# A branch hint for ScalarE at the jump past the general path

## The chip, the cores and the metric

The kernel runs on one core of a Trainium2 chip. The metric is the device time of one execution in microseconds, the median over runs. Before the change it was 179.29 us over 3 runs (179.23 to 179.44). The engines are named as the profile names them: PE is TensorE's matrix multiply and PEld its weight load, DVE is VectorE, ACT is ScalarE, POOL is GpSimd, SP is SyncE. A "q" behind a name (ACTq, SPq) is the engine's sequencer, which issues DMAs, reads registers, waits on semaphores and branches.

## The reference

Attention over 4 batches, 8 heads, 768 positions and a head size of 64. A flag for each head says whether it sees all earlier positions or only the first `n_sink` and the last `window`. The result goes through a feed-forward block that takes the larger of two products.

```python
mask = np.where(retr[0, :, 0, 0, None, None], full_mask, stream_mask)
scores = np.where(mask[None, :, :, :], scores, -1000000000.0)
scores = scores - np.max(scores, axis=-1, keepdims=True)
a = np.exp(scores)
a = a / (np.sum(a, axis=-1, keepdims=True) + 1e-09)
attn = np.matmul(a, v)
...
h1 = x @ w1
h2 = x @ w2
g = np.maximum(h1, h2)
return (g @ w_out).astype(np.float32)
```

Here three of the eight flags are set, `n_sink` is 4 and `window` is 64.

## The kernel before, in words

The program holds two versions of the computation. The special one, `tile_three_full_heads`, is right when exactly three heads see all positions and the row sums of the softmax stay in a sane range. The general one, `tile_any_heads`, is right for any flags. The special path always runs. At its end it writes a verdict of 0 or 1, and the general path runs only if the verdict is 0. With the inputs here the verdict is 1, so the general path's code is in the program and is jumped over.

The head of the program (L1657 to L1680) makes mask tables on POOL. ACT starts the DMA of the eight flags into `raw` (L1578, 64 bytes), and `head_order` sorts them on DVE into `found_i` (L1603), the heads in the order in which the special path takes them. The line L1677 reads those eight numbers into registers of POOL, DVE and ACT, since these three cast `q`, `k` and `v` from a head's place that a register names. The loads of `q`, `k` and `v` themselves bring all heads, are issued by SP and need no register.

The special path then runs through the four batches in halves of 384 positions: casts, transposes, scores (L953), exponentials (L972, ACT), masks (L991, DVE), weighted sums (L1016), normalising (L1043), then the feed-forward block (L1245 and L1302 on PE, L1270 on ACT and L1272 on DVE). The order on each engine is a plan written out by hand, so nothing in it moves when an instruction is put in elsewhere.

At the end the last output rows leave in two parts: 384 columns by a DMA of SP and 128 columns by a DMA of ACT (both L1327). PE adds up a test of the row sums (L1388), and DVE turns it into `verdict` in three small instructions (L1392, L1395, L1399). All five sequencers read `verdict` into a register (L1687) and branch on it (L1690). Behind the branch each engine waits for its own last work and gives a sign. SP walks through a list of semaphore waits, one after another, for all queues and engines. A barrier of the five engines then ends the program (these waits and the barrier carry L1727 in the profile, the line that closes the program).

The length of what is jumped over differs by engine. In the program's order PE has 3,566 instructions up to its branch and 13,744 in all; DVE 433 of 3,381; POOL 134 of 276; ACT 344 of 410; SP 114 of 116. On ACT the general path is 64 exponentials of L1518, besides the semaphore waits that they need.

A branch hint is an instruction of its own (BRANCH_PREFETCH_HINT), which names a branch that comes later and says that it will be taken. In the source `mark_branch_hint_location` names it by the label of the `If`. It stands near the end of the source, but the instruction is issued at the head of the engine's program, ahead of everything else.

Of the kernel before, what the change touches and what calls it, by code (L numbers as in the profile page):

```python
# [1574 lines left out]
def head_order(nc, small, is_retrieval, H):  # L1575

    raw = small.tile([1, 2 * H], I32, name="raw")
    nc.scalar.dma_start(  # L1578
        out=raw, in_=bass.AP(tensor=_as_int32(is_retrieval, 2 * H), offset=0, ap=[[0, 1], [1, 2 * H]])
    )  # L1580
    number = small.tile([1, H], F32, name="number")
    for h in range(H):
        nc.vector.memset(number[:, h:h + 1], float(H - h))
    flag = small.tile([1, 2 * H], F32, name="flag")
    r = small.tile([1, H], F32, name="r1")
    key = small.tile([1, H], F32, name="key")
    top = small.tile([1, H], F32, name="top")
    found = small.tile([1, H], F32, name="found")
    found_i = small.tile([1, H], I32, name="found_i")
    count = small.tile([1, 1], F32, name="count")  # L1590
    vec = nc.vector
    vec.tensor_single_scalar(out=flag, in_=raw, scalar=0.0, op=ALU.not_equal)
    two = flag.rearrange("p (h two) -> p h two", two=2)
    vec.tensor_tensor(out=r, in0=two[:, :, 0], in1=two[:, :, 1], op=ALU.max)
    vec.scalar_tensor_tensor(
        out=key, in0=r, scalar=2.0 * H, in1=number, op0=ALU.mult, op1=ALU.add
    )
    vec.max(out=top, in_=key)
    vec.tensor_scalar(
        out=key, in0=top, scalar1=2.0 * H, scalar2=-2.0 * H, op0=ALU.is_gt, op1=ALU.mult  # L1600
    )
    vec.tensor_tensor(out=key, in0=key, in1=top, op=ALU.add)
    vec.tensor_scalar(  # L1603
        out=found_i, in0=key, scalar1=-1.0, scalar2=float(H), op0=ALU.mult, op1=ALU.add
    )
    vec.tensor_reduce(out=count, in_=r, op=ALU.add, axis=AX.X)
    return found_i, count


def mask_table(nc, bias, n_sink, window):  # L1610

    at = lambda i, n=1: bias[:, 128 * i:128 * (i + n)]

    def put(i, n, base, by_key, by_query, fill=-1e30):
        nc.gpsimd.affine_select(
            out=at(i, n).rearrange("p (n c) -> p n c", c=128), in_=at(i, n).rearrange("p (n c) -> p n c", c=128),
            pattern=[[0, n], [by_query, 128]], compare_op=ALU.is_ge, fill=fill, base=base,
            channel_multiplier=by_key,
        )
    put(7, 1, 0, -1, 1)  # L1620
    put(0, 1, n_sink - 1, -1, 0)
    put(1, 2, window - 129, 1, -1)
    put(2, 1, -n_sink, 1, 0, 0.0)
    put(3, 3, window - 1, 1, -1)
    put(3, 1, -n_sink, 1, 0, 0.0)
    put(3, 3, 0, -1, 1)
    nc.gpsimd.tensor_copy(out=at(6)[0:64], in_=at(0)[0:64])
    nc.gpsimd.tensor_copy(out=at(6)[64:128], in_=at(1)[64:128])


@with_exitstack
def kernel(
    ctx: ExitStack,
    tc: tile.TileContext,
    q: bass.AP,
    k: bass.AP,
    v: bass.AP,
    is_retrieval: bass.AP,
    n_sink: int,
    window: int,  # L1640
    moe_w1: bass.AP,
    moe_w2: bass.AP,
    moe_w_out: bass.AP,
    out: bass.AP,
):
    nc = tc.nc
    B, H, S, D = q.shape
    n_sink, window = int(n_sink), int(window)
    assert D == 64 and S == 768 and H == 8
    ctx.enter_context(tc.manual_schedule())  # L1650
    anyhow = (q, k, v, is_retrieval, moe_w1, moe_w2, moe_w_out, out, n_sink, window)
    if not (1 <= window <= 64 and 0 <= n_sink <= 64):
        tile_any_heads(tc, *anyhow)
        return

    with tc.tile_pool(name="consts", bufs=1) as consts:
        tab = consts.tile([128, 16 * 128], BF16, name="tab")  # L1657
        lds = consts.tile([128, NLD, 3, H, S // 2 * D // 128], F32, name="ld")
        warm = consts.tile([128, 1], F32, name="warm")
        rez = consts.tile([128, B * H * S // 128], F32, name="rez")  # L1660
        verdict = consts.tile([1, 1], I32, name="verdict")
        warmer = consts.tile([128, 128], BF16, name="warmer")
        nc.gpsimd.memset(warmer, 0.0)
        nc.vector.memset(tab[:, 0:1152], 0.0)
        nc.gpsimd.affine_select(
            out=tab[:, 0:128], in_=tab[:, 0:128], pattern=[[1, 128]], compare_op=ALU.not_equal, fill=1.0,
            base=0, channel_multiplier=-1,
        )
        mask_table(nc, tab[:, 128:1152], n_sink, window)
        if K_BY_ACT:  # L1670
            nc.scalar.dma_start(
                out=lds[:, 0, 1], in_=k[0, :, 0:S // 2, :].rearrange("h (p n) d -> p h (n d)", p=128)
            )
        found, count = head_order(nc, consts, is_retrieval, H)
        nc.vector.memset(warm, 0.0)
        nc.scalar.activation(out=warm, in_=warm, func=ACT.Exp)
        _, heads = nc.values_load_multi_w_load_instructions(  # L1677
            found, engines=[nc.gpsimd.engine, nc.vector.engine, nc.scalar.engine], min_val=0, max_val=H - 1,
            skip_runtime_bounds_check_because="a permutation of the heads",
        )  # L1680
        tile_three_full_heads(
            tc, q, k, v, moe_w1, moe_w2, moe_w_out, out, tab, heads, rez, count,
            verdict, warmer, K_BY_ACT, lds,
        )
        tc.mark_branch_hint_location("other", hint="LikelyTaken",
            engines=[nc.tensor.engine, nc.vector.engine, nc.gpsimd.engine])
        right = nc.values_load(  # L1687
            verdict, min_val=0, max_val=1, skip_runtime_bounds_check_because="a product of two flags"
        )
    with tc.If(right < 1, label="other"):  # L1690
        tile_any_heads(tc, *anyhow)
# [40 lines left out]
```

## Time and profile before

| what | value |
|---|---|
| median of 3 runs | 179.29 us (179.23 to 179.44) |
| the profiled execution's own time | 179.4 us |
| its span, first to last instruction | 177.7 us |
| mean granted TensorE clock | 0.995 |
| DVE busy | 117.0 us (66%), 326 instructions |
| ACT busy | 124.5 us (70%), 279 instructions |
| POOL busy | 32.5 us (18%), 80 instructions |

The profiled execution took 1.7 us more than its span, and it lies 0.1 us above the median of the runs. Busy time counts only work in the engines themselves; a sequencer's waits, register reads and branches are not in it, but the views that list one source line show them with their durations and start times. Such a row reads: line, engine, operation, count, then shortest, median and longest duration in ns, then the start of the first and of the last in us.

### The profile page before, as it was taken

The numbers are of one execution on the slowest core, as the hardware profiler recorded it, in microseconds if no ns is written. First come the engines' busy times: TensorE is split into PE (matmuls) and PEld (weight loads), VectorE is DVE, ScalarE is ACT, GpSimd is POOL, SyncE is SP. The second block draws the span as 40 slices with busy tenths as digits, with TensorE's granted clock in tenths as the row PEclk, the third lists the DMA queues.
The fourth block names the chain that finished last, engine by engine and source line by source line (L and its number), as shares of the span: only waits on it lengthen the run. The fifth ranks groups of instructions, "written<-read, shape, count | busy, mean of one in ns | idle before, by whom it ended". The sixth has DMA issues, their size and how long they took to land.

```text
span 177.7 us, 4887 instructions
## 1 busy us (share of the span) xinstructions
PE 169.6 (95%) x1781; PEld 102.6 (58%) x1781; DVE 117.0 (66%) x326; ACT 124.5 (70%) x279; POOL 32.5 (18%) x80
## 2 busy tenths in 40 slices
PE   7999999999999999999999999999999999999970
PEld 7855655655756656666566447555554566545440
DVE  5448799878898787776777175786855578503130
ACT  3598716999698999999996879948475877132210
POOL 6860200320427310071001122000030000000000
PEclk9999999999999999999999999999999999999998
DMA  5999999999899998995959997549993261333040
GB/s 133 334 373 386 392 375 325 221 309 281 217 251 246 267 310 214 243 247 74 154 117 250 209 186 196 71 115 223 226 252 71 66 220 66 76 131 118 4 160 28
DMA packets 76654, 36.14 MB, mean 203 GB/s; under 512 B 59090, under 2 KB 70610, under 8 KB 76626
## 3 DMA queue, kind: packets, MB, share of 16 engines
q1 hardware_dynamic: 76480, 35.73, 78.5%
q8 instruction: 15, 0.25, 0.6%
q14 instruction: 13, 0.11, 0.2%
q10 hardware_dynamic: 146, 0.07, 0.1%
HBM read 25.17 MB, written 6.29 MB: 177 GB/s over the span
## 4 chain that ended last, share of the span: by engine, by line
PE 78%; DMA 7%; DVE 5%; ACT 2%; POOL 2%; issue 2%; DVEq 0%; SPq 0%; POOLq 0%; ACTq 0%
PE ps L1302 34%; PE ps L1245 21%; PE ps L953 9%; PE ps L1016 7%; DMA ld<-in_moe_w_out_dram 6%; PE ps L1222 3%; PE ps L674 3%; DVE at L991 1%; ACT at L972 1%; PE ps L1142 1%; POOL qb L378 1%; DMA raw<-in_is_retrieval_dram 1%; ACT wob L376 1%; POOL tab L606 1%; DVE vx L378 1%
## 5 line engine op out<-in xcount | busy, mean ns | idle before, releaser
L972 ACT ACTIVATE at<-ps 128x512 bf16<-128x512 f32 (+2 forms) x134 | 64.0, 576 | 6.7 <-PE ps L953 6.4
L1302 PE MATMUL ps<-wob,g 128*128 128x512 bf16 (+2 forms) x200 | 45.7, 371 | 0.0
L1245 PE MATMUL ps<-xt,w 128*128 128x384 bf16 x256 | 45.2, 326 | 0.0
L1245 PEld LDWEIGHTS <-w 128*128 128x128 bf16 x256 | 24.1, 98 | 16.5 <-issue 0.6
L991 DVE TENSOR_TENSOR at<-at,tab 128x1024 bf16<-128x1024 bf16 (+5 forms) x49 | 24.7, 519 | 12.4 <-ACT at L972 11.8
L1302 PEld LDWEIGHTS <-g 128*128 128x128 bf16 x200 | 18.2, 98 | 19.4 <-issue 0.2
L1272 DVE TENSOR_SCALAR g<-ps 128x384 bf16<-128x384 f32 x31 | 16.9, 552 | 14.7 <-PE ps L1245 14.3
L1302 PE MATMUL ps<-w2o,xt 128*128 128x512 bf16 (+2 forms) x100 | 24.7, 371 | 0.0
L1270 ACT ACTIVATE g<-ps 128x384 bf16<-128x384 f32 x33 | 15.9, 509 | 12.0 <-PE ps L1245 11.9
L1043 DVE TENSOR_TENSOR x<-ps,rez 128x192 f32 x64 | 22.6, 354 | 1.6
L378 POOL CAST qb<-ld 128x384 bf16 (+1 forms) x28 | 12.4, 476 | 57.3 <-DVE x L1043 19.8
L1016 PEld LDWEIGHTS <-at 128*128 128x128 bf16 x477 | 18.0, 97 | 6.1 <-DVE at L991 1.0
L376 ACT COPY ot<-ps 128x512 f32<-128x512 f32 (+1 forms) x16 | 9.1, 576 | 16.4 <-PE ps L1302 15.4
L1016 PE MATMUL ps<-vb,at 128*128 128x65 bf16 x387 | 19.3, 193 | 0.3 <-DVE at L991 0.2
L953 PE MATMUL ps<-qk 64*128 64x128 bf16 (+1 forms) x330 | 19.1, 228 | 0.0
L953 PEld LDWEIGHTS <-qk 64*128 64x128 bf16 x330 | 12.1, 94 | 9.3 <-issue 7.0
L376 ACT CAST qb<-ld 128x384 bf16 (+1 forms) x35 | 13.7, 451 | 4.5 <-DMA ld<-in_q_dram 3.3
L1302 PEld LDWEIGHTS <-xt 128*128 128x128 bf16 x100 | 8.9, 98 | 8.1
L378 DVE COPY qk<-ps 128x384 bf16<-128x384 bf16 (+1 forms) x14 | 9.6, 696 | 4.0 <-PE ps L674 3.6
L378 POOL CAST vb<-ld 128x192 bf16 x18 | 6.3, 385 | 28.7 <-DMA ld<-in_v_dram 26.6
L378 DVE COPY ot<-ps 128x512 f32<-128x512 f32 (+1 forms) x9 | 6.1, 673 | 8.0 <-PE ps L1302 8.0
L674 PE MATMUL ps<-tab,qb 128*128 128x128 bf16 x120 | 9.6, 219 | 0.5 <-POOL qb L378 0.3
(76 smaller groups left out, 162.9 us busy)
## 6 DMA issues: line engine op xcount, KB each, us to landing
out_dram<-ot SPq DMA_DIRECT2D x23, 256.0 KB, 2.6
ld<-in_v_dram SPq DMA_DIRECT2D x21, 256.0 KB, 5.2
ld<-in_moe_w_dram SPq DMA_DIRECT2D x4, 1024.0 KB, 12.1
ld<-in_q_dram SPq DMA_DIRECT2D x5, 768.0 KB, 8.2
ld<-in_k_dram SPq DMA_DIRECT2D x5, 768.0 KB, 7.8
ld<-in_q_dram SPq DMA_DIRECT2D x9, 256.0 KB, 5.1
ld<-in_k_dram SPq DMA_DIRECT2D x9, 256.0 KB, 4.6
ld<-in_moe_w_out_dram SPq DMA_DIRECT2D x4, 512.0 KB, 11.0
```

The costliest lines, as they stand in the source:

```text
L376: nc.scalar.copy(out=out, in_=in_)
L378: eng[e].tensor_copy(out=out, in_=in_)
L674: nc.tensor.transpose(to[:, i], qbs[:, T["qb", n, hf] % NQB, t, i].rearrange("p h d -> p (h d)"), ident)
L953: nc.tensor.matmul(to.rearrange("p (i c) -> p i c", c=128), lhsT=lhsT, rhs=q_of(n, i, m)[rows], start=bk not in under, stop=True, skip_gro ...
L972: nc.scalar.activation(out=at[:, bk, 0:w], in_=bank(("ps", b, hf, t), part=bk)[:, 0:w], func=ACT.Exp, scale=scale,)
L991: eng[e].tensor_tensor(out=at, in0=at, in1=tbl, op=ALU.mult)
L1016: nc.tensor.matmul(po[:, hh, i - NT * hf, :], lhsT=ats[:, T["at", b, hf, t] % NAT, bk, e * 128:(e + 1) * 128], rhs=rhs, start=first, stop= ...
L1043: nc.vector.tensor_tensor(out=xs[:, HALVES.index((b, hf)) % NX, :, bass.ds(heads[2 * p + hh], 1), :], in0=po[:, hh, :, 0:D].unsqueeze(2), ...
L1245: nc.tensor.matmul(bank(key)[:, 0:HALF], lhsT=w[:, kc, fc * 128:(fc + 1) * 128], rhs=xts[:, HALVES.index((b, hf)) % NXT, :, kc, :], start= ...
L1270: nc.scalar.activation(out=g, in_=ph, func=ACT.Relu)
L1272: nc.vector.tensor_scalar_max(out=g, in0=ph, scalar1=0.0)
L1302: nc.tensor.matmul(bank(key)[:, cols], lhsT=lhsT, rhs=(w2o if kind == "x" else wob)[:, c, cols], start=(e == 0), stop=(e == len(steps) - 1),)
```

## The change

One engine is added to the list of those that get the hint.

```diff
         tc.mark_branch_hint_location("other", hint="LikelyTaken",
-            engines=[nc.tensor.engine, nc.vector.engine, nc.gpsimd.engine])
+            engines=[nc.tensor.engine, nc.vector.engine, nc.gpsimd.engine, nc.scalar.engine])
         right = nc.values_load(
```

On ACT, at the head of the program, the order was this (the first branch enters the program; `raw` holds the flags, `warm` is a one-column tile that has the table of the exponential loaded early, `found_i` the sorted heads):

```order
L1727 UNCONDITIONAL_BRANCH
L1578 DMA raw<-in_is_retrieval_dram 1x16
L1676 ACT_TABLE_LOAD
L1676 ACTIVATE warm<-warm 128x1
L1677 TENSOR_LOAD found_i
```

And now, at the same place of ACT's program:

```order
L1727 UNCONDITIONAL_BRANCH
L1727 BRANCH_PREFETCH_HINT
L1578 DMA raw<-in_is_retrieval_dram 1x16
L1676 ACT_TABLE_LOAD
L1676 ACTIVATE warm<-warm 128x1
L1677 TENSOR_LOAD found_i
```

One instruction is new, ahead of the DMA of the flags, and everything behind it on ACT is one place later in the program. At the other end of ACT's program, where the branch itself stands, the rows are the same as before (`ot` is the last output tile):

```order
L376 COPY ot<-ps 128x128
L1327 DMA out_dram<-ot 128x128
L1687 TENSOR_LOAD verdict
L1690 COMPARE_AND_BRANCH
L1518 ACTIVATE any_a<-any_s 128x2304 x64
L1690 UNCONDITIONAL_BRANCH x2
```

Nothing moved there: ACT still jumps from the compare over the 64 exponentials. PE, DVE, POOL and SP run the same instructions in the same order as before.

## The prediction

> **What bounds the kernel now.** I looked first at where the busy time stops, then at what the sequencers do behind it. The page gives the span; the windows cut its end into pieces (each row: length, busy time and instructions of each engine, granted clock, DMA share, GB/s); the chain of waits gives the last piece of work.
>
> ```profile
> span 177.7 us, 4887 instructions
> ...
> 0.00:172.00 172.00, 169.58 (x1781) 102.59 (x1781) 116.60 (x323) 124.26 (x279) 32.50 (x80) 1.00 0.81 208
> 172.00:174.20 2.20, 0.00 (x0) 0.00 (x0) 0.43 (x3) 0.25 (x1) 0.00 (x0) 1.00 0.39 138
> 174.20:175.20 1.00, 0.00 (x0) 0.00 (x0) 0.00 (x0) 0.00 (x0) 0.00 (x0) 1.00 0.14 41
> 175.20:177.70 2.50, 0.00 (x0) 0.00 (x0) 0.00 (x0) 0.00 (x0) 0.00 (x0) 0.65 0.01 3
> ...
> 172.40 0.14 DVE verdict L1399
> ```
>
> Up to 172 us PE is busy 169.6 of 172.0, and the change touches none of that. The last work is DVE's verdict, over at 172.5. No engine computes in the 5.2 us that follow, and in the last 2.5 of them the DMAs are all but still too. So the question is what the sequencers do there. The views of the lines L1687 (register read) and L1690 (branch, and each engine's own wait behind it) show it.
>
> ```profile
> L1687 SPq TENSOR_LOAD <-verdict x1: 718/718/718, 172.6 to 172.6; - x1
> L1687 ACTq TENSOR_LOAD <-verdict x1: 555/555/555, 172.7 to 172.7; - x1
> ...
> L1690 POOLq EVENT_SEMAPHORE  x4: 17/43/43, 173.7 to 174.0; - x4
> L1690 POOLq COMPARE_BRANCH  x1: 65/65/65, 173.2 to 173.2; - x1
> L1690 DVEq COMPARE_BRANCH  x1: 84/84/84, 173.2 to 173.2; - x1
> L1690 ACTq COMPARE_BRANCH  x1: 54/54/54, 173.3 to 173.3; - x1
> L1690 SPq COMPARE_BRANCH  x1: 53/53/53, 173.4 to 173.4; - x1
> L1690 PEldq COMPARE_BRANCH  x1: 393/393/393, 173.4 to 173.4; - x1
> L1690 DVEq EVENT_SEMAPHORE  x1: 21/21/21, 173.9 to 173.9; - x1
> L1690 PEldq EVENT_SEMAPHORE  x1: 51/51/51, 173.9 to 173.9; - x1
> ...
> L1690 ACTq EVENT_SEMAPHORE  x1: 17/17/17, 176.7 to 176.7; - x1
> ```
>
> All five branch between 173.2 and 173.4. The three with a hint issue their next instruction 0.5 (POOL: 173.2 to 173.7), 0.7 (DVE) and 0.5 us (PE) later. ACT, without one, does so at 176.7, 3.4 us after its branch. It isn't held by the semaphore of that instruction: a wait shows up on ACT as a long record, as the next row says (1,913 ns for the longest), and this one is 17 ns long. ACT wasn't there yet.
>
> ```profile
> L376 ACTq EVENT_SEMAPHORE  x41: 17/17/1913, 17.8 to 170.0; - x41
> ```
>
> Who waits for ACT, the view of L1727 shows, asked for SP's walk in stretches and for the two engines that follow.
>
> ```profile
> L1727 SPq EVENT_SEMAPHORE  x12: 28/28/1912, 174.2 to 174.9; - x12
> ...
> L1727 SPq EVENT_SEMAPHORE  x1: 1912/1912/1912, 174.9 to 174.9; - x1
> ...
> L1727 SPq DRAIN  x2: 7/10/13, 176.8 to 176.9; - x2
> ...
> L1727 ACTq DRAIN  x2: 8/8/8, 176.8 to 177.1; - x2
> ...
> L1727 POOLq EVENT_SEMAPHORE  x4: 17/17/17, 176.9 to 177.6; - x4
> ```
>
> SP goes through 12 waits from 174.2 to 174.9 without a stop, 28 ns each, and stands at the twelfth for 1,912 ns, until ACT's sign at 176.7. Then come the barrier and the end, 176.8 to 177.7. So **the end is set by ACT's late return from its branch**, and by nothing else for 1.9 us.
>
> That the 3.4 us are a fetch of code is a reading of the DMA view: the page's count of instruction queues, then the stretch 172 to 178 us in 40 slices of 0.15 us, then 177 to 178 alone.
>
> ```profile
> q8 instruction: 15, 0.25, 0.6%
> q14 instruction: 13, 0.11, 0.2%
> ...
> GB/s 273 0 0 0 10 358 338 430 314 277 21 0 0 0 0 109 164 0 0 0 0 0 0 0 0 0 0 0 0 0 0 0 0 0 0 55 0 0 0 0
> ...
> q14 instruction: 4, 0.03, 1.9%
> q8 instruction: 1, 0.02, 1.0%
> ...
> q14 instruction: 1, 0.01, 3.5%
> ```
>
> The outputs flow until 173.65 (eleventh slice). At 174.25 to 174.55 (slices 16 and 17) come four packets of code, three on q14 and one on q8; a last one of q14 at 177.25 to 177.4, about 0.6 us after ACT's return. POOL, DVE and PE had been past their branch for some 0.55 us by then: theirs would be the block behind the one they landed in, as ACT's is at 177.3. The third packet of q14 at 174.3 to 174.5 has no other taker than ACT's missing target, or SP; if it is ACT's, the code is usable some 2.2 us after its packet (176.7 less 174.5).
>
> **The change, part by part.** *Removed: ACT's stop.* With the hint ACT should return like its three neighbours, 0.5 to 0.7 us after 173.3, so at 173.8 to 174.0, and give its sign there. SP asks for it at 174.9, 0.9 us later, so ACT is off the path. SP's twelfth wait shrinks from 1,912 to the 28 ns of its neighbours: 1,912 - 28 = **1.88 us**. Late next is SP's walk itself, which starts at 174.2 whatever ACT does, with the same barrier of 0.9 us behind it. No DMA takes ACT's place: the last bytes of the output are out at 173.65, and the row below has SP's last store landing 1.9 us after its issue at 171.9, at 173.8; SP has passed every wait before the twelfth without a stop.
>
> ```profile
> out_dram<-ot SPq DMA_DIRECT2D x1, 192.0 KB, 1.9
> ```
>
> *Added: one instruction at ACT's head, ahead of the DMA of the flags.* Its price is read from the three engines that have it, its cover from the start of the timeline and the register reads.
>
> ```profile
> L1727 POOLq BRANCH_PREFETCH_HINT  x1: 56/56/56, 0.8 to 0.8; - x1
> L1727 DVEq BRANCH_PREFETCH_HINT  x1: 51/51/51, 0.8 to 0.8; - x1
> ...
> 0.80 0.52 ACTq L1578 DMA_DIRECT2D raw<-in_is_retrieval_dram  x1
> ...
> 3.99 0.20 ACT L1676 ACTIVATE warm<-warm 128x1 f32<-128x1 f32 x1 [1.36 <-DVE warm L1675]
> ...
> 6.02 1.36 ACT L376 CAST qb<-ld 128x192 bf16 x5 [1.82 <-DMA ld<-in_q_dram]
> 6.02 0.35 DVE L378 CAST qb<-ld 128x192 bf16 x1 [0.84 <-DMA ld<-in_q_dram]
> ...
> L1603 DVE TENSOR_SCALAR found_i<-key x1: 160/160/160, 3.7 to 3.7; 1x8 int32<-1x8 f32 x1
> L1677 DVEq TENSOR_LOAD <-found_i x1: 841/841/841, 3.9 to 3.9; - x1
> L1677 ACTq TENSOR_LOAD <-found_i x1: 746/746/746, 4.0 to 4.0; - x1
> L1677 POOLq TENSOR_LOAD <-found_i x1: 769/769/769, 4.7 to 4.7; - x1
> ```
>
> The record is 51 to 56 ns; with a gap of the same size I estimate 0.05 to 0.11 us by which the flags land later, and `found_i` with them. Behind that DMA on ACT stand the table load, with 1.36 us of idle time after it, and the register read. DVE and ACT have their registers at 4.7 to 4.8 and then wait for `q`, which SP loads, until 6.02: 0.84 us of idle time on DVE, 1.82 on ACT. POOL reads its registers at 4.7, though `found_i` is ready at 3.9, because its own queue holds it: 0.8 us of room. So 0.11 us vanishes in 0.8, and I count it at **nothing**; without the cover it would cost its 0.11.
>
> *Moved:* every ACT instruction stands one place further in its blocks of code. ACT's sequential fetches are in q14's 13 blocks already; one more instruction among several hundred moves where a block begins, not how many there are. I count that at nothing; one stop like that at the branch (3.4 us) is its upper end, and a rival below.
>
> *Sum.* Profiled execution: 179.4 - 1.88 + 0 = 177.5, with a span of 175.8. It lies 0.1 above the median of the runs, so the median goes to 179.29 - 1.88 = **177.4**. With the head's cost and the spread of the runs (0.2) this case alone runs from 177.2 to 177.7.
>
> [...]
>
> **The rivals.** *The block behind the target comes too late.* POOL, DVE and PE ask for the next block about 0.55 us after they land (packets at 174.3 to 174.5), and by ACT's measure it is usable at 176.7. Now nobody needs it before, since all wait for SP until 176.8. Afterwards the barrier runs from 175.0 to 175.8, and an engine whose last few instructions cross into a new block would stop until 176.7. If it needs the block at 175.0, the gain is 0.1 to 0.2 (179.1); if at 175.7, it is 0.9 (178.4). Against it: about five instructions are left on each engine, and a block of q14 holds about (4,887 - 2 x 1,781) / 13 = 100 records. That is some 5% per engine; a tenth in all.
>
> *The hint does nothing for ACT.* If the 3.4 us were not a fetch, or the hinted block were pushed out in the 172 us between hint and branch, the time stays at 179.3. Against it: DVE and PE carry their hint as long and return at once. I give it 9%. [...]
>
> *Slower: the hint takes the place of ACT's next block.* If a pending hint made ACT fetch the target where it needs the following block, ACT would stop 3.4 us at one of its block boundaries in the middle, where exponentials feed PE. It decides from a stop of over 1.9 us that PE can't bridge: 179.3 - 1.9 + 3.4 = 180.8. Against it: POOL and DVE carry the hint through the whole run, and PE is still busy 169.6 of 172 us. 4%.
>
> *More than the span.* 1.7 us of the time lie outside the span, and ACT's late block at 177.3 falls near its end. If the end of the execution waits for it too (177.3 + 2.2 = 179.5), it would afterwards be there at 176.7, and the time would fall by 2.8 to 176.5. I know of no row that shows it: 4%.
>
> **How the numbers follow.** The forecast has 73%, the late block 10%, no effect 9%, slower 4%, more gain 4%. About 0.2% (0.36 us) is what a measurement of this kernel can tell from no change. Faster: 73 + 4 + the better half of the late block, 6, so 0.83. Same: 9 + 4 = 0.13. Slower: 0.04. The range reaches up to the middle of the late block's case, 178.9, and a little below the forecast's own end, 177.0; outside stay no effect, slower, the biggest gain and the rest of the late block, 2 in 10.
>
> **What would show it.** Right: ACT's instruction behind its branch (L1690) starts at 173.8 to 174.0 and not at 176.7; no wait of SP (L1727) is over 0.1 us; the barrier ends at 175.8; the register reads of L1677 move by 0.1 at most; the first casts stay at 6.0. The late block would show as a gap of about 1 us in one engine's L1727 rows with SP's walk already over. A useless hint would leave the 1.9 us in SP's row. The slower case would show a gap of over 3 us on ACT, ended by nothing that the profile names. The prediction fails if the return of ACT takes longer than 1.5 us, or if another wait of SP stops in its place.

## The result, and the profile after

The changed kernel takes 178.08 us (median of 6 runs, 177.66 to 178.15) against 179.43 us for the kernel before (6 runs, 179.23 to 180.28). The ratio is 0.9908, with a 95% interval of 0.9886 to 0.993: 1.35 us faster by the medians, where 1.88 were forecast. The time lies in the forecast range (177.0 to 178.9), 0.7 above its likeliest value of 177.4.

The tail first. The rows below are the changed kernel's: its span, the last piece of the chain of waits, the view of the branch line (L1690), then that of L1727 for SP and for ACT.

```profile
span 176.4 us, 4866 instructions
...
172.95 0.14 DVE verdict L1399
...
L1690 POOLq EVENT_SEMAPHORE  x4: 17/43/43, 174.3 to 174.5; - x4
L1690 POOLq COMPARE_BRANCH  x1: 65/65/65, 173.8 to 173.8; - x1
L1690 DVEq COMPARE_BRANCH  x1: 84/84/84, 173.8 to 173.8; - x1
L1690 ACTq COMPARE_BRANCH  x1: 68/68/68, 173.9 to 173.9; - x1
...
L1690 ACTq EVENT_SEMAPHORE  x1: 17/17/17, 174.4 to 174.4; - x1
...
L1727 SPq EVENT_SEMAPHORE  x14: 17/28/28, 174.7 to 176.3; - x14
...
L1727 ACTq BRANCH_PREFETCH_HINT  x1: 60/60/60, 0.8 to 0.8; - x1
```

ACT is back 0.5 us after its branch (173.9 to 174.4; before, 3.4 us), and the longest of SP's waits is 28 ns (before, 1,912). From the verdict to the end of the span it is 176.4 - 172.95 = 3.4 us, where it was 177.7 - 172.4 = 5.3: **the tail is 1.9 us shorter**, as forecast.

But the verdict itself comes at 172.95 us, 0.55 later than in the profile before. The difference is there early. These are DVE's first casts of the second piece of `w2`, before and then after (start, length, engine, line, operation; in brackets the idle time ahead and what ended it):

```profile
17.16 1.29 DVE L378 CAST w2b<-ld 128x1024 bf16<-128x1024 f32 x2 [0.25 <-DMA ld<-in_moe_w_dram]
```

```profile
17.75 1.30 DVE L378 CAST w2b<-ld 128x1024 bf16<-128x1024 f32 x2 [0.92 <-DMA ld<-in_moe_w_dram]
```

The load landed 0.6 us later, PE waits 0.84 us for the cast instead of 0.17, and nothing later makes up for that. Whether the hint does it, or whether executions differ in this way anyhow, is what most of the experiments are about. For the first stood two mechanisms: the flags come later, or ACT's code is shifted by one place and its fetches fall beside other loads.

The head of the program after the change, from the timeline and the views of L1592 (the first use of the flags) and L1677:

```profile
0.89 0.53 ACTq L1578 DMA_DIRECT2D raw<-in_is_retrieval_dram  x1
...
5.97 0.35 ACT L376 CAST qb<-ld 128x192 bf16 x1 [1.57 <-DMA ld<-in_q_dram]
...
L1592 DVE TENSOR_SCALAR flag<-raw x1: 282/282/282, 2.2 to 2.2; 1x16 f32<-1x16 int32 x1
...
L1677 ACTq TENSOR_LOAD <-found_i x1: 756/756/756, 4.2 to 4.2; - x1
L1677 POOLq TENSOR_LOAD <-found_i x1: 767/767/767, 4.7 to 4.7; - x1
```

The DMA of the flags is issued 0.09 us later and they are used at 2.2 instead of 2.0. ACT's register read moves by 0.2, more than the 0.1 that the prediction allowed, POOL's not at all, and the first casts start at 5.97, no later than before.

### The profile page after: what moved, and what is told of

Its sections match the earlier page's. It is cut to its first block, busy times and chain, and to the rows that moved or that the text cites. A ratio compares the mean times of both kernels' runs of the same rounds, so it can differ in the third digit from the quotient of the medians.

```text
span 176.4 us, 4866 instructions
## 1 busy us (share of the span) xinstructions
PE 167.4 (95%) x1759; PEld 102.1 (58%) x1781; DVE 116.8 (66%) x326; ACT 124.5 (71%) x279; POOL 32.5 (18%) x80
## 4 chain that ended last, share of the span: by engine, by line
PE 77%; DMA 7%; DVE 6%; issue 2%; ACT 2%; POOL 2%; DVEq 0%; SPq 0%; POOLq 0%; ACTq 0%
PE ps L1302 33%; PE ps L1245 22%; PE ps L953 8%; PE ps L1016 7%; DMA ld<-in_moe_w_out_dram 7%; PE ps L1222 3%; PE ps L674 3%; DVE at L991 1%; ACT at L972 1%; DVE qk L378 1%; PE ps L1142 1%; POOL qb L378 1%; DMA raw<-in_is_retrieval_dram 1%; DVE g L1272 1%; ACT wob L376 1%
## 5 line engine op out<-in xcount | busy, mean ns | idle before, releaser
L1302 PE MATMUL ps<-wob,g 128*128 128x512 bf16 (+2 forms) x194 | 44.6, 370 | 0.4 <-DVE kx L378 0.2
L1302 PE MATMUL ps<-w2o,xt 128*128 128x512 bf16 (+2 forms) x88 | 23.9, 370 | 0.6
```

Source lines behind the costliest of these rows:

```text
L1302: nc.tensor.matmul(bank(key)[:, cols], lhsT=lhsT, rhs=(w2o if kind == "x" else wob)[:, c, cols], start=(e == 0), stop=(e == len(steps) - 1),)
```

## The experiments

Each run was timed against the kernel before on the same chip, and one of its executions profiled in full.

### The changed kernel again (a_again)

No edit.

> The changed kernel again, nothing edited. Its tail was shorter by 1.9 us as forecast, but the time fell by only 1.35, because the loads of the head ended 0.6 us later in the profiled execution (first cast of the second piece of w2 at 17.75 instead of 17.16 us). Theory 1, the head: the hint delays the flags by 0.09 us at issue and 0.2 at landing, and that shifts the loads each time. Then the median stays at 178.0 to 178.2 and this profile shows the 17.7 again. Theory 2, spread: the end of those loads differs from execution to execution whatever the head does. Then this profile may show 17.2 as well as 17.7, and over more runs the median lies between 177.5 and 178.1, with the gain nearer to 1.6 to 1.9.

Measured: 178.11 us (6 runs, 177.77 to 178.21), ratio 0.9922 (0.9898 to 0.9947). The gain stays at 1.4 us by the medians (179.49 before), as theory 1 had it. But the load that was late in the first profile is not late in this one:

```profile
17.11 1.30 DVE L378 CAST w2b<-ld 128x1024 bf16<-128x1024 f32 x2 [0.53 <-DMA ld<-in_moe_w_dram]
```

The hint stands ahead of the flags in this execution too, so this row speaks for spread and against theory 1. It doesn't explain the time: the verdict comes at 172.75 all the same, 0.2 earlier than in the first profile and 0.35 later than before the change. Over all fourteen profiles this cast starts between 17.07 and 17.75 us, and the verdict doesn't follow it alone (17.25 and 173.17 in b_act1, 17.11 and 172.75 here).

### Flags that come late, without a hint on ACT (dose)

```diff
+        spare = consts.tile([1, 2 * H], I32, name="spare")
+        nc.scalar.dma_start(
+            out=spare, in_=bass.AP(tensor=_as_int32(is_retrieval, 2 * H), offset=0, ap=[[0, 1], [1, 2 * H]])
+        )
         found, count = head_order(nc, consts, is_retrieval, H)
```

> The kernel before (no hint on ACT), with a second 64-byte DMA of the flags into a spare tile issued on ACT ahead of the real one, so that the flags come about 0.5 us later, five times the hint's delay. Theory 1 (late flags shift the loads of the head): the body gets at least 0.4 us longer, the time 179.8 to 180.3. Theory 2 (spread; 0.8 us of room behind the flags hides it): within 0.2 us of the kernel before, 179.2 to 179.6, with the tail as before.

Measured: 179.87 us (12 runs, 179.38 to 181.39), ratio 1.0023 (1.0002 to 1.0044). The dose was far larger than meant, as its view of L1592 shows:

```profile
L1592 DVE TENSOR_SCALAR flag<-raw x1: 164/164/164, 4.7 to 4.7; 1x16 f32<-1x16 int32 x1
...
  DMA raw<-in_is_retrieval_dram: 3.0, 1
```

The flags were used at 4.7 us, 2.7 later than before, which uses up the 0.8 us of room more than three times. The median of 179.87 falls into the range of theory 1, but that range was meant for a delay of 0.5 us. Five times as much raised the median by only 0.4 us. (The execution that was profiled is the longest of the twelve, 181.39 us, and has its verdict at 174.31.) That the hint's 0.2 us, which stay within the room, should cost more is unlikely, though this run alone doesn't exclude it.

### The hint taken from DVE (swap)

```diff
-            engines=[nc.tensor.engine, nc.vector.engine, nc.gpsimd.engine, nc.scalar.engine])
+            engines=[nc.tensor.engine, nc.gpsimd.engine, nc.scalar.engine])
```

> The changed kernel with the hint taken from DVE: PE, POOL and ACT keep theirs. Theory of the fetch: DVE now returns 3.2 to 3.5 us after its branch instead of 0.6, SP stops about 1.7 to 2.0 us at a wait for DVE, and the time goes back to 179.5 to 180.2 (178.1 + 1.8). Rival (the stop was something of ACT alone): DVE returns as before, and the time stays at 178.1.

Measured: 180.03 us (12 runs, 179.7 to 180.55), ratio 1.0033 (1.0011 to 1.0055). Its views of L1690 and L1727:

```profile
L1690 DVEq COMPARE_BRANCH  x1: 72/72/72, 173.8 to 173.8; - x1
L1690 ACTq COMPARE_BRANCH  x1: 68/68/68, 173.9 to 173.9; - x1
...
L1690 ACTq EVENT_SEMAPHORE  x1: 17/17/17, 174.4 to 174.4; - x1
...
L1690 DVEq EVENT_SEMAPHORE  x1: 21/21/21, 177.4 to 177.4; - x1
...
L1727 SPq EVENT_SEMAPHORE  x14: 17/28/2177, 174.7 to 178.4; - x14
```

DVE now returns 3.6 us after its branch and SP waits 2.2 us for it. ACT, with its hint, returns at once. So the stop is not a thing of ACT, a hint removes it, and one engine's stop is enough to lose the whole gain.

### A hint for SP too (five)

```diff
-            engines=[nc.tensor.engine, nc.vector.engine, nc.gpsimd.engine, nc.scalar.engine])
+            engines=[nc.tensor.engine, nc.vector.engine, nc.gpsimd.engine, nc.scalar.engine, nc.sync.engine])
```

> The changed kernel with the hint on SP as well. SP jumps over next to nothing, yet its next instruction comes 0.8 us after its branch, where the hinted engines take 0.5 to 0.6, and its walk is now the bound. If that is a fetch in part, SP starts its walk 0.2 to 0.3 us earlier and the time falls by as much, to 177.8. If it is only the second branch that SP executes, the walk starts as before and the time is 178.1; the hint ahead of SP's first loads may then cost 0.1, to 178.2.

Measured: 177.92 us (6 runs, 177.69 to 178.85), ratio 0.9928 (0.99 to 0.9957), so no difference from the changed kernel that these runs can tell (178.11 beside it). The branch of SP and the start of its walk:

```profile
L1690 SPq COMPARE_BRANCH  x1: 68/68/68, 173.5 to 173.5; - x1
...
L1690 POOLq INC_SWDGE_SEM  x1: 175/175/175, 174.2 to 174.2; - x1
...
L1727 SPq EVENT_SEMAPHORE  x14: 17/28/28, 174.3 to 175.9; - x14
```

SP starts its walk 0.8 us after its branch as before, hint or not, and 0.1 us after POOL's last step has begun. That last distance is 0.12 to 0.13 us in all fourteen profiles, also in the run with no hints, below, where POOL is 3 us later. So SP waits for POOL there, not for code, though no row names what it waits for.

### The kernel before again (b_again)

No edit.

> The kernel before again, nothing edited, for a second profile of its head and tail. In its first profile the verdict came at 172.40 us and the tail took 5.30; four profiles with a hint on ACT have the verdict at 172.57 to 172.96 and (where every engine has its hint) a tail of 3.40. Theory of spread: this execution's verdict falls anywhere in 172.3 to 173.0. Theory that one more instruction on ACT itself costs body time: it is 172.3 to 172.5 again. The tail: 5.2 to 5.4, with ACT's stop of 3.3 to 3.5.

Measured: 179.98 us (12 runs, 179.41 to 180.61), ratio 1.0017 (0.9993 to 1.004) against 23 runs of the same program, 179.6. The verdict came at 172.75, not at 172.40 as in the first profile: two executions of the same program differ by 0.35 here. The rows, from its chain and from L1690 and L1727:

```profile
172.75 0.14 DVE verdict L1399
...
L1690 ACTq COMPARE_BRANCH  x1: 54/54/54, 173.7 to 173.7; - x1
...
L1690 ACTq EVENT_SEMAPHORE  x1: 17/17/17, 177.5 to 177.5; - x1
...
L1727 SPq EVENT_SEMAPHORE  x14: 17/28/2386, 174.5 to 178.4; - x14
```

ACT's stop lasted 3.8 us and SP waited 2,386 ns, so the tail was 178.5 - 172.75 = 5.7 us. Both are longer than expected (3.3 to 3.5 and 5.2 to 5.4): the stop differs between executions too.

### One more instruction on ACT, no hint (b_act1)

```diff
+        spare = consts.tile([128, 1], F32, name="spare")
+        for n_spare in range(1):
+            nc.scalar.activation(out=spare[:, n_spare:n_spare + 1], in_=warmer[:, 0:1], func=ACT.Exp)
         nc.vector.memset(warm, 0.0)
```

> The kernel before, without a hint on ACT, and with one more tiny activation (128x1, a spare tile) on ACT in its idle time behind the table load at 2.7 to 4.0 us. The flags are not delayed; only ACT's code moves by one place. With the hint, ACT's fetch of code that stood at 33.0 us in the first profile stands at 31.7, beside the loads of k that PE waits for from 32 to 34. Theory of the moved fetch: here too it stands near 31.7, the first k cast near 33 us comes 0.2 to 0.4 later, and the time is 179.7 to 180.0 (0.3 to 0.4 over the kernel before). Theory of spread, or of late flags: the same time as the kernel before within 0.15.

Measured: 180.09 us (12 runs, 178.89 to 180.42), ratio 1.0012 (0.9988 to 1.0036), beside 179.98 (b_again) and 179.6 (23 runs) for the unchanged kernel on the same chip. Against the first it is the same within 0.15, against the second 0.5 slower, so the time alone doesn't decide. The first casts of k on POOL do, in b_again and then here:

```profile
33.37 1.23 POOL L378 CAST qb<-ld 128x192 bf16 x4 [1.65 <-DMA ld<-in_k_dram]
```

```profile
33.40 1.23 POOL L378 CAST qb<-ld 128x192 bf16 x4 [1.79 <-DMA ld<-in_k_dram]
```

The fetch moved from 32.8 to 31.8 us, and the casts stayed within 0.03 us, where 0.2 to 0.4 were expected of a moved fetch.

### Eight more instructions on ACT, with the hint (a_act8)

The same edit in the changed kernel, with a spare tile of eight columns and `range(8)`.

> The changed kernel with eight such tiny activations on ACT behind the table load, which moves the fetch of code further ahead, to 27 to 30 us. Theory of the moved fetch: the k loads are clear of it and the body is shorter by 0.2 to 0.4 than in the changed kernel, 177.7 to 177.9, unless the fetch now meets the q loads before 30.9, which would cost as much. Theory of spread: 178.0 to 178.2 like the changed kernel.

Measured: 178.1 us (6 runs, 177.41 to 178.9), ratio 0.9912 (0.988 to 0.9945): the changed kernel's time. ACT's fetch went further than expected, to 21.5 us instead of 27 to 30, well clear of the k loads. The profile has the earliest verdict of all, though the hint is on ACT:

```profile
172.32 0.14 DVE verdict L1399
```

With the run before and short_act1 below, this leaves nothing that shows for the moved fetch.

### No hints at all (none)

```diff
-        tc.mark_branch_hint_location("other", hint="LikelyTaken",
-            engines=[nc.tensor.engine, nc.vector.engine, nc.gpsimd.engine])
```

> The hint taken from all engines; nothing else changed. Theory of the fetch with stops side by side: PE, DVE, POOL and ACT each return 3.2 to 3.7 us after their branch, at 176.6 to 177.2; SP stops once, for 1.7 to 2.4 us in all, and the time is 179.5 to 180.2, hardly more than with ACT alone unhinted. Theory that the stops add up (one queue for the code of four engines): returns up to 1.5 us later still, 180.7 to 181.5.

Measured: 181.29 us (6 runs, 180.78 to 181.53), ratio 1.008 (1.0048 to 1.0111), 1.1 above the range expected of stops side by side and inside that of stops that add up. The rows (the branch is L1688 and the end L1725 here) show neither theory as it was put:

```profile
L1688 POOLq EVENT_SEMAPHORE  x4: 17/43/43, 177.0 to 177.3; - x4
L1688 POOLq COMPARE_BRANCH  x1: 45/45/45, 173.5 to 173.5; - x1
L1688 DVEq COMPARE_BRANCH  x1: 72/72/72, 173.6 to 173.6; - x1
L1688 ACTq COMPARE_BRANCH  x1: 54/54/54, 173.6 to 173.6; - x1
L1688 SPq COMPARE_BRANCH  x1: 53/53/53, 173.7 to 173.7; - x1
L1688 PEldq COMPARE_BRANCH  x1: 3393/3393/3393, 173.7 to 173.7; - x1
L1688 ACTq EVENT_SEMAPHORE  x1: 17/17/17, 174.1 to 174.1; - x1
L1688 PEldq EVENT_SEMAPHORE  x1: 51/51/51, 177.2 to 177.2; - x1
L1688 DVEq EVENT_SEMAPHORE  x1: 21/21/21, 177.3 to 177.3; - x1
L1688 POOLq INC_SWDGE_SEM  x1: 177/177/177, 177.4 to 177.4; - x1
...
L1725 SPq EVENT_SEMAPHORE  x14: 17/28/28, 177.5 to 179.1; - x14
```

POOL, PE and DVE stop for 3.5 to 3.7 us, side by side. SP, which starts behind POOL as always, begins its walk only at 177.5, so the walk no longer runs under the stop as it did before but comes after it. That makes the tail 6.4 us instead of 5.3, and another 0.3 us lies outside the span (2.0 instead of 1.7). And ACT, without a hint, returns 0.5 us after its branch. So the missing hint alone did not make ACT stop in the kernel before.

### A short general path (short, short_act1, short_hint) and the changed kernel beside it (a_again2)

The general path is cut to one batch of four and four heads of eight in all three. The first has no hint on ACT, the second has besides one activation as in b_act1, the third has the hint.

```diff
-    for b in range(B):
+    for b in range(1):
...
-        for h in range(H):
+        for h in range(4):
```

> The kernel before, no hint on ACT, but with a much shorter general path: it leaves out three of its four batches and four of its eight heads (it is jumped over with these inputs, and would be incomplete if it ran). ACT jumps over 8 exponentials and their waits instead of 64. Theory A (ACT's stop is a fetch because the place behind the path is not in the block that comes next): the place is near now, ACT returns 0.4 to 0.6 us after its branch without any hint, the tail is 3.4 us, and the time 177.6 to 178.2. Theory B (an unhinted engine stops whatever it jumps over, where others have a hint): 3.3 to 3.9 us, tail 5.3 to 5.7, 179.4 to 180. Where A holds, this kernel has the short tail without a new instruction on ACT. Spread then gives it the changed kernel's time within 0.15; a cost of the hint itself in the body makes it 0.3 to 0.5 faster (177.6 to 177.8).

> The kernel with the shortened general path, no hint on ACT, and one tiny activation on ACT behind the table load (as in the earlier run with one): only ACT's code moves by one place. If the moved fetch costs body time, 0.2 to 0.4 slower than the shortened kernel without it; otherwise the same within 0.15.

> The changed kernel (hint on ACT) with the shortened general path. The tail needs no hint here, so what the hint costs at the head is left alone: with late flags or a moved fetch, 0.2 to 0.5 slower than the shortened kernel without it; by spread, the same within 0.15.

> The changed kernel once more, beside the shortened ones on the same chip: 178.0 to 178.2, tail 3.40, verdict between 172.5 and 173.1.

Measured, all on one chip beside 179.68 us for the kernel before (17 runs):

| kernel | hint on ACT | median us (lowest to highest, runs) | ratio (interval) |
|---|---|---|---|
| short | no | 178.2 (177.68 to 178.89, 9) | 0.9925 (0.9897 to 0.9953) |
| short_act1 | no | 178.2 (177.84 to 178.64, 8) | 0.9922 (0.9896 to 0.9947) |
| short_hint | yes | 178.26 (177.58 to 178.42, 6) | 0.9911 (0.9877 to 0.9945) |
| a_again2 | yes | 178.18 (177.74 to 178.75, 7) | 0.9916 (0.9885 to 0.9947) |

The rows of short:

```profile
173.23 0.14 DVE verdict L1399
```

```profile
L1690 ACTq COMPARE_BRANCH  x1: 54/54/54, 174.2 to 174.2; - x1
...
L1690 ACTq EVENT_SEMAPHORE  x1: 17/17/17, 174.6 to 174.6; - x1
```

With the place behind the path near, ACT returns 0.4 us after its branch without a hint: theory A. The four medians lie within 0.1 us of each other. Since short has the short tail with neither late flags nor shifted code, and short_hint has both, this pair is the test of what the hint costs in the body: 0.06 us between the medians, where the intervals are about half a microsecond wide to either side. No cost shows. None of the twelve runs was faster than the changed kernel by more than these intervals.

## Why the prediction was right, and where it was off

**What bounds the end.** Right. SP's wait for ACT was the end of the program, and with it gone SP's walk (from 174.7 us, no wait over 28 ns) and the barrier follow at once, to the end at 176.4.

**The removed stop, 1.88 us.** Right in the profile: SP's row went from 1,912 to 28 ns, the tail from 5.3 to 3.4. ACT returned 0.5 us after its branch, the lower end of the forecast 0.5 to 0.7. Its time of day was off, 174.4 instead of 173.8 to 174.0, only because the verdict was late.

**The hint's cost at the head, nothing.** Right. The instruction took 60 ns, the flags came 0.2 us later (0.05 to 0.11 were estimated; in b_again, without the hint, they are used at 2.2 as well), and the first casts did not move (5.97 us, before 6.02). short and short_hint differ by 0.06 us, within the noise. The shift of ACT's code costs nothing that shows either (the k casts of b_act1, and short_act1).

**The sum, 177.4.** Here is the term that was mis-sized: the body. The sum took the 172.4 us up to the verdict from one profile as if every execution had them. Seven profiles with a hint on ACT have the verdict at 172.32, 172.57, 172.75, 172.75, 172.95, 172.96 and 173.16, mean 172.8. Six without one, the dose apart, have it at 172.40, 172.71, 172.75, 172.75, 173.17 and 173.23, mean 172.8 as well. So no difference of the body with and without the hint shows, it spreads over 0.9 us, and the first profile had a short one. With 172.8, the tail of 3.4 and the 1.7 us around the span, the sum is 177.9, near the measured 178.08 to 178.18. That the time still lies in the range is luck in part: the forecast's own case ended at 177.7, and the range went up to 178.9 for the late block, which did not happen.

What the runs leave open is the other side. With the same body and the tails seen in four profiles without the cure (5.3, 5.7, 5.3, and 5.3 in the dose), the kernel before should take 172.8 + 5.3 + 1.7 = 179.8 or more. Its medians were 179.43 to 179.68 in four groups of runs and 179.98 in b_again. Against b_again the gain is the forecast 1.9 us (a_act8, on the same chip, 178.1), against the other groups 1.35 to 1.5. Its shortest execution took 178.6, less than the earliest verdict seen plus the usual tail plus 1.7 us (172.32 + 5.3 + 1.7 = 179.3). In some executions either the body or ACT's stop must be shorter than in any that was profiled in full. I didn't see one, so why the gain is mostly 1.35 to 1.5 us and not 1.9 is shown only in part.

**That the stop is a fetch.** The prediction took ACT's row of 17 ns as a sign that ACT was late and not held, and the third early packet of q14 as ACT's missing target. Neither is safe alone: SP in none goes on only 3.8 us after its branch, in step with POOL, and its row shows 28 ns as well; and three early packets of q14 come after the change too. What bears the reading out is the number of all packets of code. These are the counts of whole executions for the changed kernel, swap and none:

```profile
q8 instruction: 15, 0.25, 0.6%
q14 instruction: 12, 0.10, 0.2%
```

```profile
q8 instruction: 15, 0.25, 0.6%
q14 instruction: 13, 0.11, 0.2%
```

```profile
q8 instruction: 16, 0.26, 0.6%
q14 instruction: 14, 0.11, 0.2%
```

Before the change it was 15 and 13. All the difference lies behind the branch: four packets in the eight profiles in which no engine stopped, five in the five in which one did, and seven in none, with three stopped. Each stopped engine has one more packet of code fetched, and the late packet comes 0.6 to 0.9 us after an engine's return (before the change at 177.3, after 176.7; in swap at 178.0, after 177.4).

**Why ACT stopped.** The prediction said: because it had no hint. The runs show that this is half of it. Without a hint PE, DVE and POOL, which jump over 10,178, 2,948 and 142 instructions in the program's order, stop 3.5 to 3.7 us (none). For DVE the hint alone makes the difference: with it it returned after 0.6 us (173.8 to 174.4, changed kernel), without it after 3.6 (173.8 to 177.4, swap). ACT has 66 to jump over; it stopped in every profile of the kernel before, yet not in none (back after 0.5 us), where ACT runs the same instructions in the same order, and not in short (0.4 us). The hints of the other engines are the difference between the first two. How they act on ACT stays open; no row shows it.

**The rivals.** A useless hint is refuted. So is the slower case: no stop shows in ACT's middle, where its longest waits are for PE, 4.7 and 3.5 us, as before, and the bodies agree. The late block did not show: the four packets of code behind the branch started at 174.9 to 175.0, and in the walk and the barrier that followed no wait of SP was over 28 ns. More gain than the span's did not come: time less span stayed 1.7 us (178.07 - 176.4).

## What to carry to other kernels

- Look at the sequencers behind the last computed result: waits, branches and the barrier are busy time nowhere, and here they were 5.3 us of 179. A branch hint took 50 to 60 ns at the head and cost nothing that showed, while the slowest return from the branch (3.4 us, ACT's) set the end. So an engine whose code is jumped over belongs on the list or must be seen to return promptly (0.4 to 0.7 us here).
- Don't take the body's length from one execution. Where a gain is 1% and the loads of the head land half a microsecond apart from run to run (17.07 to 17.75 us for one cast here), two profiles mix both, and a pair of kernels that differ in the disputed cost alone tells them apart.

## What was not expected of the hardware

- The same unhinted jump of ACT stopped it for 3.4 us (before) and 3.8 us (b_again) where PE, DVE and POOL had the hint, and not at all where none had it (back after 0.5 us, none).
- A 64-byte load as the second one in ACT's queue was used 2.7 us later than as the first (4.7 instead of 2.0 us), though only one issue of about 0.5 us stood ahead of it; by then SP had issued the large load of `q` (768 KB, issued from 0.80 to 1.26 us in the profile before).
- With no hints the execution took 2.0 to 2.1 us more than its span, in all six runs, where the other kernels have 1.7 to 1.9. Code was fetched there as late as 178.2 us, 0.9 before the span's end.
- Each branch's record shows its hint: 68 ns with it and 54 without on ACT, 84 and 72 on DVE, 65 and 45 on POOL.
- The hint's own fetch shows nowhere. Between the start of the span and the branch there are 14 packets of code on q8 and 9 on q14 with hints on no engine, on three or on four (8 on q14 with five). When the code of a hinted engine came can't be read from these traces.
